# A decode block on one core: the second part of a late V is mixed one step later, and the down projection's weights lie in K's buffer

## The chip, the cores and the metric

The kernel runs on one core of one Trainium2 chip. The metric is the device time of an execution in microseconds (us); the kernel before took 1325.12 us in the median of three runs (1320.38 to 1325.15). The engines named below are TensorE (PE), VectorE (DVE), ScalarE (ACT) and SyncE (SP); nearly all transfers are issued from SP's queue, in program order.

## What is computed

One token for each of two sequences goes through a pre-norm attention block with a cache of 8192 keys and values in 16 heads of 256, and then through a gated projection without a nonlinearity:

```
# x: [2, 1, 448]; k_cache, v_cache: [2, 16, 8192, 256]; float32
q = layernorm(x) @ wq                        # 16 heads x 256
p = softmax(einsum("bhqd,bhkd->bhqk", q, k_cache) * 256 ** -0.5)
h = x + einsum("bhqk,bhkd->bhqd", p, v_cache) @ wo
n = layernorm(h)
out = h + ((n @ w_gate) * (n @ w_up)) @ w_down     # 448 -> 1792 -> 448
```

K and V of one head of one sequence are 8.39 MB each (8192 x 256 x 4 bytes), and there are 32 such pairs; all inputs together are 561 MB.

## The kernel before

**Tiling.** A pair i = 2 * head + sequence is one unit. The 8192 keys lie as 128 partitions x 64 rows (NJ = 64) of 256 elements, so a row of the buffer is 0.131 MB, and "16 rows" below are 2.10 MB. `k_sb` holds 112 rows: an even pair's K stands in rows 0 to 63, an odd pair's in rows 48 to 111. Both use rows 48 to 63, and every pair's `scores` begins with those 16 rows (for an even pair by taking part (part - 1) mod 4), so the next K may be loaded when the first of four parts has been reduced. `v_sb` holds a single V, 64 rows.

**A step.** The loop runs over n = 0 to 32. Step n loads V of pair n-1 and K of pair n+1, computes the scores of pair n, and the softmax and the mix (weights times V) of pair n-1. In program order: `load_v(n-1)`; `scores(n, 0)`, which multiplies 16 rows of K by q on DVE in place, calls `softmax(n-1)`, and then reduces those rows; `load_k(n+1)`; the other loads of V; a load of weights `w` in one step of four; `scores(n, 1)`, `norm(n-1)`, `scores(n, 2)` and `scores(n, 3)`; `mix(n-1)` and `mixed(n-1)`; `top(n)`. Each engine does its own instructions in this order; semaphores order them between engines.

**The pieces, with their lines.** `scores` is a product (L243) and a reduction (L246) on DVE for each of four parts. `top` takes the maximum over a row on DVE (L251) and transposes it on PE (L253, `mT`). `softmax` takes the maximum over the transposed row on DVE (L257, `nm`), spreads it by a matmul (L259), and makes the weights `p` and their sums on ACT (L264), which a matmul adds up (L268). `mix` is 32 matmuls (L279; each shows as two instructions in the profile) that add into one of two PSUM tiles `o_ps`, taken in turn; each reads two rows of V. `mixed` copies `o_ps` (ACT, L288), turns it into a column (PE, L292), scales it (ACT, L298) and, for the second sequence of a head, adds the output projection (PE, L301).

**The late steps.** For the last five pairs V is loaded in parts, by the table `LATE`: pair 27 in 56 + 8 rows, 28 in 48 + 16, 29 and 30 in 32 + 32, and 31 in 32 + 16 + 8 + 8. The first part is issued at the start of the step, the others behind `load_k(n+1)`.

**The end.** After the loop the gate's weights `wg` and the up projection's `wu` (3136 KB each) are loaded into rows of `k_sb`, and the down projection's `wd` into rows of `v_sb`, in three pieces (1792, 896 and 448 KB; L357). `project` multiplies the normed h by `wg` and by `wu` (both L379), and L438 multiplies by `wd` into `y_ps`, which DVE copies (L444) and two transfers store.

Of the kernel before, what the change touches and what calls it, by code (L numbers as in the profile page):

```python
# [13 lines left out]
B, D, H, SK, DH, F = 2, 448, 16, 8192, 256, 1792  # L14
# [5 lines left out]
NJ = SK // P  # L20
# [10 lines left out]
NF = F // P  # L31
# [13 lines left out]
def tile_decode_block(  # L45
# [8 lines left out]
    wd: bass.AP,  # L54
    out: bass.AP,
):

# [87 lines left out]
    def load_w(hp, lo=0, hi=WQ + 2 * WO):  # L147

        t = wpool.tile([P, WQ + 2 * WO], F32, tag="w", name=f"w_{hp}_{lo}")
        nc.sync.dma_start(t[:, lo:hi], w[hp][:, lo:hi])  # L150
        return t

    k_sb = const.tile([P, 2 * NJ - OVER, DH], F32, name="k_sb")
    v_sb = const.tile([P, NJ, DH], F32, name="v_sb")

    def keys_of(cache, i, lo, hi):
        h, b = divmod(i, B)
        return cache[b, h].rearrange("(p j) d -> p j d", p=P)[:, lo:hi, :]

    def k_at(i, lo, hi):  # L160
        base = i % 2 * (NJ - OVER)
        return k_sb[:, base + lo : base + hi, :]

    def load_k(i, lo=0, hi=NJ):
        nc.sync.dma_start(k_at(i, lo, hi), keys_of(k_cache, i, lo, hi))

    def load_v(i, lo=0, hi=NJ):
        nc.sync.dma_start(v_sb[:, lo:hi, :], keys_of(v_cache, i, lo, hi))
# [36 lines left out]
    def queries(hp, w):  # L205

        got = []
        for b in range(B):
            ps = ps_q.tile([P, 2 * DH], F32, tag="q", name=f"q_ps_{hp}_{b}")
            for c in range(DC - 1):  # L210
                nc.tensor.matmul(  # L211
                    ps, xb[:, c, b, :], w[:, c * 2 * DH : (c + 1) * 2 * DH],
                    start=(c == 0), stop=False,
                )
            for k in range(2):
                nc.tensor.matmul(  # L216
                    ps[:, k * DH : (k + 1) * DH], xb[:, DC - 1 + k, b, :],
                    w[:, 3 * 2 * DH : WQ], start=False, stop=(k == 1),
                )
            q = qpool.tile([P, 2, DH], F32, tag="q", name=f"q_{hp}_{b}")  # L220
            nc.scalar.activation(  # L221
                q.rearrange("p h d -> p (h d)"), ps, AF.Copy, scale=rstd[:, b : b + 1]
            )
            got.append(q)
        return got


    NQ = H * B
# [3 lines left out]
    def scores(i, part, between=None):  # L232

        h, b = divmod(i, B)
        if part == 0:
            s_t[i] = work.tile([P, NJ], F32, tag="s", name=f"s_{i}")

        lo = (part - 1) % (NJ // HC) * HC if i % 2 == 0 else part * HC  # L240
        kt = k_at(i, lo, lo + HC)
        q = q_t[h // 2][b][:, h % 2, :]
        nc.vector.tensor_mul(kt, kt, q[:, None, :].to_broadcast([P, HC, DH]))  # L243
        if between is not None:
            between()
        nc.vector.tensor_reduce(s_t[i][:, lo : lo + HC], kt, axis=AX.X, op=ALU.add)  # L246

    def top(i):

        m = work.tile([P, 1], F32, tag="m", name=f"m_{i}")  # L250
        nc.vector.tensor_reduce(m, s_t[i], axis=AX.X, op=ALU.max)  # L251
        mT_t[i] = ps_s.tile([1, P], F32, tag="sm", name=f"mT_{i}")
        nc.tensor.transpose(mT_t[i], m, ident)  # L253

    def softmax(i):
        nm = work.tile([1, 1], F32, tag="nm", name=f"nm_{i}")
        nc.vector.tensor_reduce(nm, mT_t[i], axis=AX.X, op=ALU.max, negate=True)  # L257
        nb_ps = ps_s.tile([P, 1], F32, tag="sm", name=f"nb_ps_{i}")
        nc.tensor.matmul(nb_ps, row, nm, start=True, stop=True)  # L259
        nb = work.tile([P, 1], F32, tag="nb", name=f"nb_{i}")  # L260
        nc.scalar.activation(nb, nb_ps, AF.Copy)  # L261
        p_t[i] = work.tile([P, NJ], F32, tag="p", name=f"p_{i}")
        lsum = work.tile([P, 1], F32, tag="lsum", name=f"lsum_{i}")
        nc.scalar.activation(  # L264
            p_t[i], s_t[i], AF.Exp, bias=nb, scale=DH**-0.5, accum_out=lsum
        )
        l_t[i] = ps_s.tile([P, 1], F32, tag="sm", name=f"l_ps_{i}")
        nc.tensor.matmul(l_t[i], ones, lsum, start=True, stop=True)  # L268

    def norm(i):  # L270
        rl_t[i] = work.tile([P, 1], F32, tag="rl", name=f"rl_{i}")
        nc.vector.reciprocal(rl_t[i], l_t[i])

    def mix(i):

        o, p = o_ps[i % 2], p_t[i]
        for t in range(NJ // 2):
            g = 32 * (t % 4)
            nc.tensor.matmul(  # L279
                o[g : g + 2, :], p[:, 2 * t : 2 * t + 2], v_sb[:, 2 * t : 2 * t + 2, :],  # L280
                start=(t < 4), stop=(t >= NJ // 2 - 4),
            )

    def mixed(i):

        h, b = divmod(i, B)
        o_sb = work.tile([P, 2 * DH], F32, tag="o_sb", name=f"o_sb_{i}")
        nc.scalar.activation(o_sb, o_ps[i % 2], AF.Copy)  # L288
        oT_ps = ps_s.tile([P, 2], F32, tag="sm", name=f"oT_ps_{i}")
        for c in range(2):  # L290
            for k in range(2):
                nc.tensor.matmul(  # L292
                    oT_ps[:, c : c + 1], o_sb[:, (2 * k + c) * P : (2 * k + c + 1) * P],
                    sel[:, k : k + 1], start=(k == 0), stop=(k == 1),
                )
        if b == 0:
            oT_t[h] = work.tile([P, 2, B], F32, tag="oT", name=f"oT_{h}")
        nc.scalar.activation(oT_t[h][:, :, b], oT_ps, AF.Copy, scale=rl_t[i])  # L298
        if b == B - 1:
            for c in range(2):  # L300
                nc.tensor.matmul(  # L301
                    acc_ps, oT_t[h][:, c, :], wo_t[h][:, c * D : (c + 1) * D],
                    start=(h == 0 and c == 0), stop=(h == H - 1 and c == 1),
                )

    for part in FIRST:
        load_k(0, *part)
    for n in range(NQ + 1):
        hp, at = divmod(n, 2 * B)
        late = n - 1 - (NQ - len(LATE))  # L310
        parts, todo = (LATE[late] if late >= 0 else (NJ,)) if n > 0 else (), []
        for k in range(len(parts)):
            todo.append((n - 1, sum(parts[:k]), sum(parts[: k + 1])))
        if n > 0:
            load_v(*todo.pop(0))
        if n < NQ:
            scores(n, 0, (lambda: softmax(n - 1)) if n > 0 else None)
        else:
            softmax(n - 1)
        if n + 1 < NQ:  # L320
            load_k(n + 1)
        for v in todo:
            load_v(*v)
        if at == 1:
            last = hp + 1 == H // 2
            t = load_w(hp + 1, lo=WQ, hi=WQ + WO) if last else load_w(hp + 1)
            w_t[hp + 1] = t
            for k in range(2):
                wo_t[2 * hp + k] = t[:, WQ + k * WO : WQ + (k + 1) * WO]
        if n == NQ:  # L330
            nc.sync.dma_start(wo_t[H - 1], w[H // 2][:, WQ + WO :])
        if n < NQ:
            scores(n, 1)
        if n > 0:
            norm(n - 1)
        if n < NQ:
            for part in range(2, NJ // HC):
                scores(n, part)
        if n > 0:
            mix(n - 1)  # L340
            mixed(n - 1)
        if at == 2 and hp + 1 < H // 2:
            q_t[hp + 1] = queries(hp + 1, w_t[hp + 1])
        if n < NQ:
            top(n)


    wg_t, wu_t = (
        k_sb.rearrange("p j d -> p (j d)")[:, k * NF * D : (k + 1) * NF * D] for k in range(2)
    )  # L350
    nc.sync.dma_start(wg_t, wg)
    nc.sync.dma_start(wu_t, wu)

    wd_t = v_sb.rearrange("p j d -> p (j d)")[:, : NF * D].rearrange("p (n d) -> p n d", d=D)
    at = 0
    for n in (8, 4, 2):
        nc.sync.dma_start(  # L357
# [150 lines left out]
```

## Time and profile before

| what | before |
|---|---|
| median of the runs | 1325.12 us |
| lowest and highest run | 1320.38, 1325.15 us |
| the profiled execution's own time | 1325.09 us |
| its span, first to last instruction | 1322.9 us |
| PE busy | 489.7 us (37%) |
| DVE busy | 1144.6 us (87%) |
| ACT busy | 62.3 us (5%) |
| bytes read, mean rate | 561.19 MB, 424 GB/s |
| mean granted clock of PE | 0.652 |

The profile is of one execution. In a row of the timeline the columns are the start, the time of one or of a merged run of instructions, the engine (SPq is SP issuing a transfer), the line, the operation, what it writes and reads, the count, and in brackets the idle time of that engine ahead of it with what ended it. In a row of the table by stretches there follow on the stretch and its length: busy time of PE, its weight loads, DVE, ACT and GpSimd, the granted clock of PE (1.00 is full), the busy share of the 16 DMA engines and the rate in GB/s. A row of a transfer gives its size and the time from its issue to its landing.

### The profile page before, as it was taken

Reading aid. Unit: us, or ns where it says so; the run is one execution under the profiler, and the core shown is the slowest. Engines: PE = TensorE matmul, PEld = TensorE weight load, DVE = VectorE, ACT = ScalarE, POOL = GpSimd, SP = SyncE. Lnnn points to the kernel's source line nnn. Section 1 sums busy time; section 2 is a strip of 40 time slices with the busy share of each in tenths; the row PEclk is TensorE's granted clock in tenths of the full one; section 3 lists DMA queues with packets and bytes.
Section 4 is the critical chain, followed back from the end, with each engine's and each line's share of the span. In section 5 each row is a group of like instructions: output and inputs, shape, how many; then the busy total and the mean of one; then the engine's idle time right before and its main releaser. Section 6 shows DMA issues by size and latency. Waiting matters only on the chain.

```text
span 1322.9 us, 6801 instructions
## 1 busy us (share of the span) xinstructions
PE 489.7 (37%) x2936; PEld 166.8 (13%) x2936; DVE 1144.6 (87%) x394; ACT 62.3 (5%) x183; POOL 1.2 (0%) x8
## 2 busy tenths in 40 slices
PE   3126333163331434324243451235332253243237
PEld 2012010020110211001010110012100020011013
DVE  7997999979998799897999989987999979979691
ACT  1000000000000000000000000000000000000000
POOL 0000000000000000000000000000000000000000
PEclk8567665576765866657666675667656686665668
DMA  9999999999999999999999999999999999999995
GB/s 408 444 434 421 434 440 430 428 434 439 428 431 436 438 430 429 423 450 428 434 434 430 431 438 431 432 434 429 434 439 426 433 432 433 432 392 394 424 426 219
DMA packets 12722, 561.62 MB, mean 425 GB/s; under 512 B 1427, under 2 KB 1429, under 8 KB 2069
## 3 DMA queue, kind: packets, MB, share of 16 engines
q1 hardware_dynamic: 12680, 561.19, 98.4%
q8 instruction: 23, 0.38, 0.1%
q14 instruction: 7, 0.05, 0.0%
q10 hardware_dynamic: 12, 0.01, 0.0%
HBM read 561.19 MB, written 0.00 MB: 424 GB/s over the span
## 4 chain that ended last, share of the span: by engine, by line
DMA 70%; DVE 25%; PE 4%; issue 1%; ACT 0%; SPq 0%; POOLq 0%; DVEq 0%; POOL 0%
DMA k_sb<-in_A_k_cache_dram 63%; DVE s L246 13%; DVE k_sb L243 12%; DMA v_sb<-in_A_v_cache_dram 7%; PE o_ps L279 2%; PE acc_ps L301 1%; PE oT_ps L292 0%; PE g_ps L379 0%; PE u_ps L379 0%; PE q_ps L198 0%; PE y_ps L438 0%; ACT o_sb L288 0%; DVE nm L257 0%; PE mT L253 0%; DVE xb L134 0%
## 5 line engine op out<-in xcount | busy, mean ns | idle before, releaser
L243 DVE TENSOR_TENSOR k_sb<-k_sb,q 128x4096 f32<-128x4096 f32 x128 | 564.9, 4414 | 119.7 <-DMA k_sb<-in_A_k_cache_dram 116.2
L246 DVE TENSOR_REDUCE s<-k_sb 128x16 f32<-128x4096 f32 x128 | 565.3, 4416 | 3.3
L279 PE MATMUL o_ps<-v_sb,p 128*2 128x512 f32 x2048 | 298.1, 745 | 455.2 <-DMA v_sb<-in_A_v_cache_dram 455.2
L279 PEld LDWEIGHTS o_ps<-v_sb,p 128*2 128x2 f32 x2048 | 53.7, 97 | 670.7 <-DMA v_sb<-in_A_v_cache_dram 461.7
L259 PE MATMUL nb_ps<-nm,row 1*128 1x1 f32 x64 | 16.9, 331 | 178.0 <-DVE nm L257 178.0
L253 PE MATMUL mT<-ident,m 128*1 128x128 f32 x32 | 10.7, 335 | 136.8 <-DVE m L251 136.8
L288 ACT ACTIVATE o_sb<-o_ps 128x512 f32<-128x512 f32 x32 | 19.1, 597 | 775.3 <-PE o_ps L279 775.3
L292 PE MATMUL oT_ps<-sel,o_sb 128*128 128x1 f32 x256 | 35.3, 259 | 23.2 <-ACT o_sb L288 23.2
L211 PE MATMUL q_ps<-w,xb 128*128 128x512 f32 x84 | 40.3, 616 | 0.0
L292 PEld LDWEIGHTS oT_ps<-sel,o_sb 128*128 128x128 f32 x256 | 32.6, 199 | 54.8 <-ACT o_sb L288 54.8
L301 PE MATMUL acc_ps<-w,oT 128*2 128x448 f32 x64 | 37.2, 718 | 5.6 <-ACT oT L298 5.6
L259 PEld LDWEIGHTS nb_ps<-nm,row 1*128 1x128 f32 x64 | 14.7, 283 | 187.2 <-issue 109.7
L268 PE MATMUL l_ps<-lsum,ones 128*128 128x1 f32 x64 | 17.9, 349 | 23.5 <-ACT p L264 23.5
L257 DVE TENSOR_REDUCE nm<-mT 1x1 f32<-1x128 f32 x32 | 8.7, 272 | 19.5 <-PE mT L253 19.5
L261 ACT ACTIVATE nb<-nb_ps 128x1 f32<-128x1 f32 x32 | 5.5, 171 | 351.0 <-PE nb_ps L259 351.0
L253 PEld LDWEIGHTS mT<-ident,m 128*1 128x1 f32 x32 | 2.6, 82 | 148.0 <-DVE m L251 114.2
L211 PEld LDWEIGHTS q_ps<-w,xb 128*128 128x128 f32 x84 | 16.1, 200 | 21.8 <-issue 21.4
L268 PEld LDWEIGHTS l_ps<-lsum,ones 128*128 128x128 f32 x64 | 15.2, 295 | 26.2 <-ACT p L264 26.2
L216 PE MATMUL q_ps<-w,xb 128*128 128x256 f32 x56 | 14.4, 379 | 0.0
L389 DVE TENSOR_TENSOR h_sb<-x_sb,acc_ps 2x448 f32<-2x448 f32 x1 | 0.6, 607 | 14.1 <-PE acc_ps L301 14.1
L221 ACT ACTIVATE q<-q_ps,rstd 128x512 f32<-128x512 f32 x14 | 9.6, 687 | 61.9 <-PE q_ps L216 61.9
L216 PEld LDWEIGHTS q_ps<-w,xb 128*128 128x128 f32 x56 | 10.6, 190 | 7.4 <-issue 6.7
(78 smaller groups left out, 100.4 us busy)
## 6 DMA issues: line engine op xcount, KB each, us to landing
v_sb<-in_A_v_cache_dram SPq DMA_DIRECT2D x5, 4096.0 KB, 23.2
w<-in_w_dram SPq DMA_DIRECT2D x7, 1792.0 KB, 33.7
v_sb<-in_A_v_cache_dram SPq DMA_DIRECT2D x1, 7168.0 KB, 27.6
v_sb<-in_A_v_cache_dram SPq DMA_DIRECT2D x1, 6144.0 KB, 29.6
k_sb<-in_A_k_cache_dram SPq DMA_DIRECT2D x2, 2048.0 KB, 13.5
k_sb<-in_A_k_cache_dram SPq DMA_DIRECT2D x1, 4096.0 KB, 22.8
v_sb<-in_A_v_cache_dram SPq DMA_DIRECT2D x2, 2048.0 KB
k_sb<-in_B_w_gate_dram SPq DMA_DIRECT2D x1, 3136.0 KB, 22.1
```

Source lines behind the costliest of these rows:

```text
L211: nc.tensor.matmul(ps, xb[:, c, b, :], w[:, c * 2 * DH : (c + 1) * 2 * DH], start=(c == 0), stop=False,)
L216: nc.tensor.matmul(ps[:, k * DH : (k + 1) * DH], xb[:, DC - 1 + k, b, :], w[:, 3 * 2 * DH : WQ], start=False, stop=(k == 1),)
L221: nc.scalar.activation(q.rearrange("p h d -> p (h d)"), ps, AF.Copy, scale=rstd[:, b : b + 1])
L243: nc.vector.tensor_mul(kt, kt, q[:, None, :].to_broadcast([P, HC, DH]))
L246: nc.vector.tensor_reduce(s_t[i][:, lo : lo + HC], kt, axis=AX.X, op=ALU.add)
L253: nc.tensor.transpose(mT_t[i], m, ident)
L259: nc.tensor.matmul(nb_ps, row, nm, start=True, stop=True)
L268: nc.tensor.matmul(l_t[i], ones, lsum, start=True, stop=True)
L279: nc.tensor.matmul(o[g : g + 2, :], p[:, 2 * t : 2 * t + 2], v_sb[:, 2 * t : 2 * t + 2, :], start=(t < 4), stop=(t >= NJ // 2 - 4),)
L288: nc.scalar.activation(o_sb, o_ps[i % 2], AF.Copy)
L292: nc.tensor.matmul(oT_ps[:, c : c + 1], o_sb[:, (2 * k + c) * P : (2 * k + c + 1) * P], sel[:, k : k + 1], start=(k == 0), stop=(k == 1),)
L301: nc.tensor.matmul(acc_ps, oT_t[h][:, c, :], wo_t[h][:, c * D : (c + 1) * D], start=(h == 0 and c == 0), stop=(h == H - 1 and c == 1),)
```

## The change

Two things are changed.

First, `mix` takes a range of rows. Where a step loads its V in two parts and a K is still to come (n = 28, 29 and 30, pairs 27, 28 and 29), the step ends with the mix of the first part only, and `(pair, lo, hi)` of the second part is kept in `rest`. The next step does that second part, and `mixed` of the pair, right behind its own softmax. Step 31 loads no further K, so pair 30 is mixed whole, as before, and so is pair 31 in step 32.

Second, `wd` takes the third stretch of 14 x 448 elements a partition in `k_sb`, behind `wg` and `wu` (rows 49 to 73), in place of the first stretch of `v_sb`.

```diff
--- before.py
+++ after.py
@@ -54,6 +54,7 @@
     wd: bass.AP,
     out: bass.AP,
 ):
+
 
 
 
@@ -271,10 +272,10 @@
         rl_t[i] = work.tile([P, 1], F32, tag="rl", name=f"rl_{i}")
         nc.vector.reciprocal(rl_t[i], l_t[i])
 
-    def mix(i):
+    def mix(i, lo=0, hi=NJ):
 
         o, p = o_ps[i % 2], p_t[i]
-        for t in range(NJ // 2):
+        for t in range(lo // 2, hi // 2):
             g = 32 * (t % 4)
             nc.tensor.matmul(
                 o[g : g + 2, :], p[:, 2 * t : 2 * t + 2], v_sb[:, 2 * t : 2 * t + 2, :],
@@ -305,6 +306,7 @@
 
     for part in FIRST:
         load_k(0, *part)
+    rest = None
     for n in range(NQ + 1):
         hp, at = divmod(n, 2 * B)
         late = n - 1 - (NQ - len(LATE))
@@ -317,6 +319,13 @@
             scores(n, 0, (lambda: softmax(n - 1)) if n > 0 else None)
         else:
             softmax(n - 1)
+        if rest is not None:
+            mix(*rest)
+            mixed(rest[0])
+            rest = None
+
+        if todo and n + 1 < NQ:
+            rest = todo[0]
         if n + 1 < NQ:
             load_k(n + 1)
         for v in todo:
@@ -337,21 +346,23 @@
             for part in range(2, NJ // HC):
                 scores(n, part)
         if n > 0:
-            mix(n - 1)
-            mixed(n - 1)
+            mix(n - 1, 0, rest[1] if rest is not None else NJ)
+            if rest is None:
+                mixed(n - 1)
         if at == 2 and hp + 1 < H // 2:
             q_t[hp + 1] = queries(hp + 1, w_t[hp + 1])
         if n < NQ:
             top(n)
 
 
-    wg_t, wu_t = (
-        k_sb.rearrange("p j d -> p (j d)")[:, k * NF * D : (k + 1) * NF * D] for k in range(2)
+
+    wg_t, wu_t, wd_t = (
+        k_sb.rearrange("p j d -> p (j d)")[:, k * NF * D : (k + 1) * NF * D] for k in range(3)
     )
     nc.sync.dma_start(wg_t, wg)
     nc.sync.dma_start(wu_t, wu)
 
-    wd_t = v_sb.rearrange("p j d -> p (j d)")[:, : NF * D].rearrange("p (n d) -> p n d", d=D)
+    wd_t = wd_t.rearrange("p (n d) -> p n d", d=D)
     at = 0
     for n in (8, 4, 2):
         nc.sync.dma_start(
```

The built programs show what moves. The first place is PE between the scores of steps 28 and 29. Before, from the sum of the weights of pair 27 (`l_ps`) on; `mT` is the transpose in `top(28)`, and `o_ps_98` the PSUM tile that pair 27 adds into:

```order
L268 MATMUL l_ps_2197<-lsum_2195,ones 128x1
L279 MATMUL o_ps_98<-v_sb,p_2194 2x512 x32
L292 MATMUL oT_ps_2244<-sel,o_sb_2242 128x1 x4
L301 MATMUL acc_ps<-w_0_1975,oT_2179 2x448 x2
L253 MATMUL mT_2254<-ident,m_2252 1x128
L259 MATMUL nb_ps_2261<-nm_2259,row 128x1
L268 MATMUL l_ps_2268<-lsum_2266,ones 128x1
```

After, the same stretch:

```order
L269 MATMUL l_ps_2197<-lsum_2195,ones 128x1
L280 MATMUL o_ps_98<-v_sb,p_2194 2x512 x28
L254 MATMUL mT_2240<-ident,m_2238 1x128
L260 MATMUL nb_ps_2247<-nm_2245,row 128x1
L269 MATMUL l_ps_2254<-lsum_2252,ones 128x1
L280 MATMUL o_ps_98<-v_sb,p_2194 2x512 x4
L293 MATMUL oT_ps_2263<-sel,o_sb_2261 128x1 x4
L302 MATMUL acc_ps<-w_0_1975,oT_2179 2x448 x2
```

The last 4 matmuls of mix 27, its column turn (L292, now L293) and the output projection have moved behind the three small matmuls of pair 28's maximum and softmax.

The second place is PE in steps 30 and 31. Before, from mix 29 on; `mT_2397` belongs to `top(30)` and `mT_2466` to `top(31)`:

```order
L279 MATMUL o_ps_98<-v_sb,p_2337 2x512 x32
L292 MATMUL oT_ps_2387<-sel,o_sb_2385 128x1 x4
L301 MATMUL acc_ps<-w_1792_2273,oT_2322 2x448 x2
L253 MATMUL mT_2397<-ident,m_2395 1x128
L259 MATMUL nb_ps_2404<-nm_2402,row 128x1
L268 MATMUL l_ps_2411<-lsum_2409,ones 128x1
L279 MATMUL o_ps_97<-v_sb,p_2408 2x512 x32
L292 MATMUL oT_ps_2457<-sel,o_sb_2455 128x1 x4
L253 MATMUL mT_2466<-ident,m_2464 1x128
L259 MATMUL nb_ps_2471<-nm_2469,row 128x1
```

After, from the first part of mix 29 on; `mT_2371` belongs to `top(30)` and `mT_2466` to `top(31)`:

```order
L280 MATMUL o_ps_98<-v_sb,p_2320 2x512 x16
L254 MATMUL mT_2371<-ident,m_2369 1x128
L260 MATMUL nb_ps_2378<-nm_2376,row 128x1
L269 MATMUL l_ps_2385<-lsum_2383,ones 128x1
L280 MATMUL o_ps_98<-v_sb,p_2320 2x512 x16
L293 MATMUL oT_ps_2406<-sel,o_sb_2404 128x1 x4
L302 MATMUL acc_ps<-w_1792_2273,oT_2341 2x448 x2
L280 MATMUL o_ps_97<-v_sb,p_2382 2x512 x32
L293 MATMUL oT_ps_2457<-sel,o_sb_2455 128x1 x4
L254 MATMUL mT_2466<-ident,m_2464 1x128
```

The second 16 matmuls of mix 29, its turn and the output projection now stand in step 31, ahead of mix 30, which is whole; ahead of `mT_2466` stand 48 matmuls of L280 since the softmax, where there were 32.

The third place is the end of SP's queue. Before:

```order
L331 DMA w_1792_2273<-in_w_dram 128x896
L351 DMA k_sb<-in_B_w_gate_dram 128x6272
L352 DMA k_sb<-in_B_w_up_dram 128x6272
L357 DMA v_sb<-in_wd_dram 128x3584
L357 DMA v_sb<-in_wd_dram 128x1792
L357 DMA v_sb<-in_wd_dram 128x896
```

After:

```order
L340 DMA w_1792_2273<-in_w_dram 128x896
L362 DMA k_sb<-in_B_w_gate_dram 128x6272
L363 DMA k_sb<-in_B_w_up_dram 128x6272
L368 DMA k_sb<-in_wd_dram 128x3584
L368 DMA k_sb<-in_wd_dram 128x1792
L368 DMA k_sb<-in_wd_dram 128x896
```

The order is the same; the three pieces of `wd` go to `k_sb`. Before, they waited for the matmuls of mix 31 that read those rows of V; now they wait for reductions of pair 31's K.

## The prediction

> **What bounds the kernel now.** I read the page first, for what is busy and for the chain that ended last.
>
> ```profile
> span 1322.9 us, 6801 instructions
> q1 hardware_dynamic: 12680, 561.19, 98.4%
> DMA 70%; DVE 25%; PE 4%; issue 1%; ACT 0%; SPq 0%; POOLq 0%; DVEq 0%; POOL 0%
> L257 DVE TENSOR_REDUCE nm<-mT 1x1 f32<-1x128 f32 x32 | 8.7, 272 | 19.5 <-PE mT L253 19.5
> ```
>
> One queue moves 561 MB and is busy for 98.4% of the span, so over the whole kernel the transfers are the limit. The last row speaks against "nothing else matters": VectorE (DVE) stood 19.5 us in front of the small reduction of L257, which needs TensorE's (PE's) transpose mT. The timeline of DVE says where: the rows below open steps 29, 30 and 31 (each step's first product with K), and give L257's wait in each; the last ends the scores of step 31.
>
> ```profile
> 1160.09 4.42 DVE L243 TENSOR_TENSOR k_sb<-k_sb,q 128x4096 f32<-128x4096 f32 x1 [0.61 <-DMA k_sb<-in_A_k_cache_dram]
> 1170.90 0.28 DVE L257 TENSOR_REDUCE nm<-mT 1x1 f32<-1x128 f32 x1 [6.38 <-PE mT L253]
> 1202.10 4.42 DVE L243 TENSOR_TENSOR k_sb<-k_sb,q 128x4096 f32<-128x4096 f32 x1
> 1208.78 0.28 DVE L257 TENSOR_REDUCE nm<-mT 1x1 f32<-1x128 f32 x1 [2.26 <-PE mT L253]
> 1239.98 4.42 DVE L243 TENSOR_TENSOR k_sb<-k_sb,q 128x4096 f32<-128x4096 f32 x1
> 1254.79 0.28 DVE L257 TENSOR_REDUCE nm<-mT 1x1 f32<-1x128 f32 x1 [10.40 <-PE mT L253]
> 1285.85 0.22 DVE L251 TENSOR_REDUCE m<-s 128x1 f32<-128x64 f32 x1
> ```
>
> 6.38 + 2.26 + 10.40 = 19.04 us, all in the steps whose V comes in two parts. PE's timeline gives the cause: mixes (L279) that wait for V.
>
> ```profile
> 1162.59 1.88 PE L279 MATMUL o_ps<-v_sb,p 128*2 128x512 f32 x8 [14.35 <-DMA v_sb<-in_A_v_cache_dram]
> 1177.10 7.24 PE L279 MATMUL o_ps<-v_sb,p 128*2 128x512 f32 x48 [4.38 <-DMA v_sb<-in_A_v_cache_dram]
> 1202.33 3.59 PE L279 MATMUL o_ps<-v_sb,p 128*2 128x512 f32 x16 [17.99 <-DMA v_sb<-in_A_v_cache_dram]
> 1213.16 6.26 PE L279 MATMUL o_ps<-v_sb,p 128*2 128x512 f32 x32 [2.08 <-DMA v_sb<-in_A_v_cache_dram]
> 1245.11 5.64 PE L279 MATMUL o_ps<-v_sb,p 128*2 128x512 f32 x32 [25.70 <-DMA v_sb<-in_A_v_cache_dram]
> 1256.55 3.62 PE L279 MATMUL o_ps<-v_sb,p 128*2 128x512 f32 x32
> 1265.70 5.59 PE L279 MATMUL o_ps<-v_sb,p 128*2 128x512 f32 x32 [5.54 <-DMA v_sb<-in_A_v_cache_dram]
> 1286.13 0.37 PE L253 MATMUL mT<-ident,m 128*1 128x128 f32 x1 [13.05 <-DVE m L251]
> 1288.76 9.44 PE L279 MATMUL o_ps<-v_sb,p 128*2 128x512 f32 x64
> ```
>
> The second parts (x8, x16, x32 at 1162.59, 1202.33, 1245.11) land only after the next K, and mT stands behind them in PE's queue. DVE's stall then delays the transfers too: K(n+1) goes into rows that DVE's first reduce of step n frees, and SP's queue shows it, since K30 and K31 were issued as those reduces ended; the third row is the second half of V30, issued when the mix that began at 1245.11 was over.
>
> ```profile
> 1175.53 0.33 SPq L165 DMA_DIRECT2D k_sb<-in_A_k_cache_dram  x1
> 1213.41 0.33 SPq L165 DMA_DIRECT2D k_sb<-in_A_k_cache_dram  x1
> 1250.83 0.33 SPq L168 DMA_DIRECT2D v_sb<-in_A_v_cache_dram  x1
> ```
>
> The table by stretches shows the queue running dry at both places; the last column is GB/s.
>
> ```profile
> 1172.00:1176.00 4.00, 0.38 (x2) 0.30 (x2) 4.00 (x2) 0.29 (x2) 0.00 (x0) 0.77 0.34 147
> 1212.00:1220.00 8.00, 6.26 (x32) 0.99 (x32) 7.96 (x3) 0.00 (x0) 0.00 (x0) 0.59 0.76 287
> 1220.00:1304.00 84.00, 34.51 (x202) 9.45 (x202) 56.61 (x23) 3.80 (x12) 0.00 (x0) 0.67 1.00 428
> 1304.00:1308.00 4.00, 2.81 (x28) 1.58 (x32) 2.12 (x14) 0.00 (x0) 0.00 (x0) 0.91 0.73 298
> ```
>
> **The change part by part.** Nothing before 1160 moves: steps 0 to 28 load and compute as before, but for the last 8 instructions of mix 27.
>
> *DVE.* mT of steps 28, 29, 30 now stands ahead of the second part of the mix, behind a first part whose V landed long before (1177.1 and 1213.2 against scores that end near 1196 and 1232). The three stalls go. What is late next is K. K30 landed 4.9 us ahead of V28's second part (2.10 MB at 428 GB/s), so at 1202.3 - 4.9 = 1197.4. Its issue moves up 6.4 us, but V28's first part still fills the queue until 1177.1, so K30 gains only the dry spell: 0.7 to 2.6 us (below); I take 0.7, landing 1196.7. DVE alone would be ready at 1202.1 - 6.4 = 1195.7, so step 30 opens at 1196.7. A step without stall takes 1239.98 - 1202.10 - 2.26 = 35.6 us, so step 31 opens at 1232.3 (K31, 1245.1 - 9.8 = 1235.3 now, needs to come 3 us earlier; it does, by the next paragraph). Step 31 costs 1286.07 - 1239.98 - 10.40 = 35.7: scores end at **1268.0, 18.1 us earlier**.
>
> *Transfers.* The dry spells are counted in two ways. By rate against 428: 4 x (1 - 147/428) = 2.6 and 8 x (1 - 287/428) = 2.6, together 5.3. By landings: K30 and V28's second part, 10.49 MB, took 1177.1 to 1202.3 = 25.2 where 428 GB/s needs 24.5; K31 and V29's second part, 12.58 MB, took 1213.2 to 1245.1 = 31.9 where 29.4 would do: together 3.2. With K30 issued 6.4 us and K31 7.5 us earlier, both come while the queue still has V in it, so neither spell is left. I take the middle, **4.3 us**, ends 0 and 5.3 (more than the spells hold can't be won: the bytes stay).
>
> By the Trainium skill ("DMA: Bandwidth & Descriptors", Anatomy of one DMA) a transfer has about 2.0 us of fixed cost beside its bytes; two exposed starts would make an estimate of 4.0 us, and the time 0.3 us longer than mine.
>
> *PE and SP.* The second part's 8, 16 and 32 instructions cost what they did (1.9, 3.6, 5.6 us) and now lie beside DVE's reduces, with the softmax ahead of them. Queued behind them: V's next second part must wait for them. A step's product takes 4.4 us, the softmax 2.6 (mT at 1286.13 to the mix at 1288.76): V28's second part is released near 1160.1 + 4.4 + 2.6 + 1.9 = 1169.0, V29's near 1196.7 + 4.4 + 2.6 + 3.6 = 1207.3, and the queue then has K30 (to 1196.7) or K31 (to 1231.0) still moving, so that wait is covered by over 20 us. The load of w in step 29 waits for the output projection of mix 27, now near 1174, under the same cover. V30's second half is released by the mix that V29's landing starts, as before. In step 31 PE does mix 29's rest, all of mix 30 with its column turn (L292), then mT.
>
> ```profile
> 1272.02 1.05 PE L292 MATMUL oT_ps<-sel,o_sb 128*128 128x1 f32 x8 [0.73 <-ACT o_sb L288]
> ```
>
> V30's second half lands at 1265.7 - 4.3 = 1261.4; now from the mix's start at 1265.70 to the end of that turn at 1273.07 are 7.4 us, so mT stands at 1268.8: 0.8 us of new wait.
>
> *The end.* mix 31 starts 2.6 us after mT, at 1271.4, and takes 9.4, to 1280.8. With nothing else in the way it would end 17.4 us ahead of 1298.2. But V31 and the weights come last now.
>
> ```profile
> 1272.70 0.44 SPq L352 DMA_DIRECT2D k_sb<-in_B_w_up_dram  x1
> w<-in_w_dram SPq DMA_DIRECT2D x1, 448.0 KB, 14.6
> k_sb<-in_B_w_gate_dram SPq DMA_DIRECT2D x1, 3136.0 KB, 22.1
> k_sb<-in_B_w_up_dram SPq DMA_DIRECT2D x1, 3136.0 KB, 28.9
> 1311.39 4.04 PE L379 MATMUL u_ps<-k_sb,xr 128*32 128x256 f32 x62
> 1319.70 0.28 DVE L444 COPY y<-y_ps 128x112 f32<-128x112 f32 x1 [2.65 <-PE y_ps L438]
> SPq L357 <- PE o_ps L279: 18.6, 3, 17.0
> 1292.40 2.71 SPq L357 DMA_DIRECT2D v_sb<-in_wd_dram  x3
> ```
>
> The up weights landed at 1272.70 + 28.9 = 1301.6, 9.8 us before u used them. Less 4.3 they land at 1297.3. Behind V31's last part the queue has the last w, gate and up, 6.88 MB or 16.1 us, so V31 is there at 1281.2; an x8 takes 1.9, and mix 31 ends at 1283.1. From its end to u were 1311.39 - 1298.2 = 13.2 us, so PE is ready for u at 1296.3 and waits 1.0 us. From u's start to the copy of y are 8.3 us, and 3.2 to the end: 1297.3 + 8.3 + 3.2 = **1308.8**.
>
> *wd in K's rows.* It removes the 18.6 us that SP waited for mix 31, but until 1304 the queue was full (428 GB/s), so that wait cost nothing before; after it wd is issued behind the up weights at once, and its bytes end at 1304 + 2.8 - 4.3 = 1302.5, by when y needs its first part (1297.3 + 5.4). I cost it at 0. With wd still in V's rows it would be issued 3.6 us (1288.76 to 1292.40) into mix 31, at 1275, while the queue is full to 1297: no cost either, so no cover is lost.
>
> **Sum.** The profiled run took 1325.09 for a span of 1322.9, 2.2 us around it, and is the median (1325.12) itself. 1308.8 + 2.2 = **1311.0**.
>
> **Rivals.**
> - *The dry spells only move* (late V or K loads leave the same gaps elsewhere). For it: part of the lost rate may be a straggling end of a transfer. Then the up weights stay at 1301.6: 1301.6 + 11.5 + 2.2 = 1315.3. Chance 0.16.
> - *A cold PE at the end.* After idling 25.70 and 5.54 us the same x32 took 5.64 and 5.59, without idling 3.62. If PE's wait for the up weights is long enough to lose the clock, u takes 4.04 x 1.54 = 6.2: 1313.2. Against it: the wait I expect is 1 us. Chance 0.13. The Trainium skill ("TensorE: Matmul & The Clock Gate", Part 1) has the clock fall to half after an idle window of about 3.4 us, free-running; by that rule 1 us does not suffice, and the trace's 5.54 us agrees.
> - *Transfers gain as much as DVE* (a faster stretch than 428): the whole 18.5 us, 1306.6. Against it: the bytes after 1177 are unchanged. Chance 0.08.
> - *The stall comes back.* mT of step 31 behind mix 30, or K late by 10 us; or mT was not what DVE lacked: 1320 to 1325. Against it: the rows of PE above. Chance 0.09.
> - *Slower: SP is held by the moved mix.* V29's second part, and behind it all of V30, V31 and the weights, wait for the rest of mix 28. If this came free only with the softmax of step 31 (near 1239), K31's end at 1231 would leave the queue dry for some 10 us, and the same at V30's second half: 1311 + 20 = 1331. It decides from a release later than 1231; I expect 1207, so 24 us of margin. Chance 0.04.
>
> **How the numbers follow.** Forecast 0.50, the rest as above. The range 1305 to 1316.5 holds the forecast, the cold PE, the moved spells and most of the full gain, and leaves out the returning stall and the slower case, with a little of each edge. 0.5%, about what a measurement can tell here, is 6.6 us: faster is below 1318.5. Forecast and first three rivals fall there: 0.87; the returning stall is within: 0.09; slower 0.04.
>
> **What would show it.** Right: L257's waits in steps 29 to 31 gone; K30 and K31 issued near 1169 and 1206, no stretch below 400 GB/s between 1177 and 1300; the last scores near 1268; PE waiting for the up weights before u. Wrong: a wait of DVE on K of over 3 us in step 30 or 31, a dry stretch near 1231 or 1242, or a wait of PE on mT's place in step 31.

## The result, and the profile after

The changed kernel took 1311.24 us in the median of six runs (1310.35 to 1312.84) against 1325.13 us before (1320.38 to 1326.29): 13.9 us less, a ratio of 0.9905 with a 95% interval of 0.9886 to 0.9925. The runs of the kernel before lie in two groups, 1319.8 to 1321.3 and 1323.1 to 1326.3 us in all jobs, and its profile is of the upper one, so against the lower one the gain is about 9 us, and no trace tells what differs between them. The profiled run took 1310.35 us for a span of 1308.1; the forecast was 1311.0 and 1308.8.

The page of the changed kernel, in the lines shown of before (span, queue, chain by engine):

```profile
span 1308.1 us, 6800 instructions
q1 hardware_dynamic: 12680, 561.19, 99.4%
DMA 73%; DVE 23%; PE 3%; issue 0%; ACT 0%; POOLq 0%; DVEq 0%; POOL 0%
```

The same bytes fill 99.4% of a shorter span. From the waits of DVE between 1160 and 1322, the row of the reduction that had stood 19.5 us, and then DVE's timeline where steps 29, 30 and 31 open, with the end of the last scores (lines are one higher than before):

```profile
DVE nm L258 <- PE mT L254: 1.1, 1, 1.1
```

```profile
1160.04 4.42 DVE L244 TENSOR_TENSOR k_sb<-k_sb,q 128x4096 f32<-128x4096 f32 x1 [0.61 <-DMA k_sb<-in_A_k_cache_dram]
1164.38 0.27 DVE L258 TENSOR_REDUCE nm<-mT 1x1 f32<-1x128 f32 x1
1196.40 4.43 DVE L244 TENSOR_TENSOR k_sb<-k_sb,q 128x4096 f32<-128x4096 f32 x1 [0.74 <-DMA k_sb<-in_A_k_cache_dram]
1200.75 0.27 DVE L258 TENSOR_REDUCE nm<-mT 1x1 f32<-1x128 f32 x1
1231.95 4.42 DVE L244 TENSOR_TENSOR k_sb<-k_sb,q 128x4096 f32<-128x4096 f32 x1
1236.28 0.27 DVE L258 TENSOR_REDUCE nm<-mT 1x1 f32<-1x128 f32 x1
1267.35 0.22 DVE L252 TENSOR_REDUCE m<-s 128x1 f32<-128x64 f32 x1
1268.67 0.28 DVE L258 TENSOR_REDUCE nm<-mT 1x1 f32<-1x128 f32 x1 [1.10 <-PE mT L254]
```

The three stalls are gone: L258 follows its product without a bracket. What is left is 0.74 us on K30 and, at the end, 1.10 us on mT of step 31. The scores end 18.5 us earlier (1267.35 against 1285.85, the start of their last maximum), but the span shrinks by 14.8. SP's queue and the table by stretches say where the rest went:

```profile
1169.02 0.33 SPq L166 DMA_DIRECT2D k_sb<-in_A_k_cache_dram  x1
1205.38 0.33 SPq L166 DMA_DIRECT2D k_sb<-in_A_k_cache_dram  x1
1268.17 0.47 SPq L363 DMA_DIRECT2D k_sb<-in_B_w_up_dram  x1
k_sb<-in_B_w_up_dram SPq DMA_DIRECT2D x1, 3136.0 KB, 28.3
```

```profile
1172.00:1176.00 4.00, 2.51 (x4) 0.26 (x2) 3.96 (x2) 0.00 (x0) 0.00 (x0) 0.50 0.95 410
1212.00:1220.00 8.00, 6.41 (x32) 0.99 (x32) 7.96 (x4) 0.00 (x0) 0.00 (x0) 0.64 1.10 475
1220.00:1224.00 4.00, 0.00 (x0) 0.00 (x0) 4.00 (x2) 0.00 (x0) 0.00 (x0) 0.66 0.76 328
1220.00:1300.00 80.00, 47.29 (x310) 15.59 (x312) 51.46 (x35) 4.49 (x13) 0.00 (x0) 0.68 0.98 415
```

K30 and K31 are issued 6.5 and 8.0 us earlier, the two dry spells (147 and 287 GB/s) are gone (410 and 475), and the up weights land at 1268.17 + 28.3 = 1296.5, 5.1 us earlier. They can't gain as much as DVE does, since the same bytes have to be moved. Three landings, at which PE's mixes of V29's first and second part and of V30's first half begin, are used further down:

```profile
1212.16 6.41 PE L280 MATMUL o_ps<-v_sb,p 128*2 128x512 f32 x32 [3.08 <-DMA v_sb<-in_A_v_cache_dram]
1241.23 5.53 PE L280 MATMUL o_ps<-v_sb,p 128*2 128x512 f32 x32 [2.72 <-DMA v_sb<-in_A_v_cache_dram]
1250.96 3.62 PE L280 MATMUL o_ps<-v_sb,p 128*2 128x512 f32 x32 [0.40 <-DMA v_sb<-in_A_v_cache_dram]
```

The end of PE's timeline:

```profile
1280.51 1.04 PE L280 MATMUL o_ps<-v_sb,p 128*2 128x512 f32 x8 [0.98 <-DMA v_sb<-in_A_v_cache_dram]
1284.12 3.15 PE L302 MATMUL acc_ps<-w,oT 128*2 128x448 f32 x4 [0.35 <-ACT oT L299]
1290.35 1.92 PE L390 MATMUL g_ps<-k_sb,xr 128*32 128x512 f32 x8 [0.50 <-DVE xr L135]
1292.72 4.12 PE L390 MATMUL g_ps<-k_sb,xr 128*32 128x512 f32 x22
1296.56 0.41 PE L390 MATMUL u_ps<-k_sb,xr 128*32 128x256 f32 x2
1296.80 3.91 PE L390 MATMUL u_ps<-k_sb,xr 128*32 128x256 f32 x62
```

The gate's two rows before:

```profile
1306.10 1.05 PE L379 MATMUL g_ps<-k_sb,xr 128*32 128x512 f32 x8 [0.50 <-DVE xr L134]
1307.79 3.76 PE L379 MATMUL g_ps<-k_sb,xr 128*32 128x512 f32 x22
```

mix 31 ends at 1281.55, after waiting for V31's last part, and u begins right behind the gate's products (L390 into `g_ps`), its main run at 1296.8, 0.3 us behind the landing of the up weights. No bracket stands ahead of u: in this execution PE's own chain came last, but by so little that a PE ahead by more than 0.3 us would have waited for the up weights. Two limits nearly meet there.

### The profile page after: what moved, and what is told of

It reads as the page before. It is cut to its first block, busy times and chain, and to the rows that moved or that the text cites. A ratio compares the mean times of both kernels' runs of the same rounds, so it can differ in the third digit from the quotient of the medians.

```text
span 1308.1 us, 6800 instructions
## 1 busy us (share of the span) xinstructions
PE 492.3 (38%) x2936; PEld 169.0 (13%) x2936; DVE 1144.4 (87%) x394; ACT 62.3 (5%) x183; POOL 1.2 (0%) x8
## 3 DMA queue, kind: packets, MB, share of 16 engines
q1 hardware_dynamic: 12680, 561.19, 99.4%
## 4 chain that ended last, share of the span: by engine, by line
DMA 73%; DVE 23%; PE 3%; issue 0%; ACT 0%; POOLq 0%; DVEq 0%; POOL 0%
DMA k_sb<-in_A_k_cache_dram 68%; DVE k_sb L244 11%; DVE s L247 11%; DMA v_sb<-in_A_v_cache_dram 5%; PE o_ps L280 1%; PE g_ps L390 0%; PE u_ps L390 0%; PE q_ps L199 0%; PE acc_ps L302 0%; PE y_ps L449 0%; DVE nm L258 0%; PE oT_ps L293 0%; DVE xb L135 0%; DVE o_ps L102 0%; PE hm_ps L442 0%
## 5 line engine op out<-in xcount | busy, mean ns | idle before, releaser
L280 PE MATMUL o_ps<-v_sb,p 128*2 128x512 f32 x2048 | 298.2, 745 | 401.6 <-DMA v_sb<-in_A_v_cache_dram 401.6
L280 PEld LDWEIGHTS o_ps<-v_sb,p 128*2 128x2 f32 x2048 | 53.6, 97 | 616.5 <-DMA v_sb<-in_A_v_cache_dram 408.7
L293 PE MATMUL oT_ps<-sel,o_sb 128*128 128x1 f32 x256 | 35.8, 261 | 23.2 <-ACT o_sb L289 23.2
L293 PEld LDWEIGHTS oT_ps<-sel,o_sb 128*128 128x128 f32 x256 | 33.1, 202 | 54.8 <-ACT o_sb L289 54.8
L265 ACT ACTIVATE p<-s,nb 128x64 f32<-128x64 f32 x32 | 11.1, 347 | 1.0
```

The costliest lines, as they stand in the source:

```text
L265: nc.scalar.activation(p_t[i], s_t[i], AF.Exp, bias=nb, scale=DH**-0.5, accum_out=lsum)
L280: nc.tensor.matmul(o[g : g + 2, :], p[:, 2 * t : 2 * t + 2], v_sb[:, 2 * t : 2 * t + 2, :], start=(t < 4), stop=(t >= NJ // 2 - 4),)
L293: nc.tensor.matmul(oT_ps[:, c : c + 1], o_sb[:, (2 * k + c) * P : (2 * k + c + 1) * P], sel[:, k : k + 1], start=(k == 0), stop=(k == 1),)
```

## The experiments

All ratios are against runs of the kernel before in the same job. That kernel's median was 1325.13 us in the job of the result and 1323.58, 1320.52 and 1324.35 us in the three jobs below; since it moves by up to 4.6 us, a kernel's own median is given beside its ratio.

### The deferred mix alone

```diff
-wd_t = wd_t.rearrange("p (n d) -> p n d", d=D)
+wd_t = v_sb.rearrange("p j d -> p (j d)")[:, : NF * D].rearrange("p (n d) -> p n d", d=D)
```

The third stretch of `k_sb` is not taken either (not shown).

> The deferred mix alone, wd back in V's rows. Theory A (the mix does it all): 1311 us, as with both edits; wd is issued about 3.6 us into mix 31, near 1275, still ahead of the end of the up weights near 1296. Rival B (the place of wd gives part of it): 1314 us or more, with wd landing after y is ready for it.

Measured: 1310.53 us (1310.18 to 1310.92), ratio 0.9899 (0.9875 to 0.9924). SP's row for wd in that run:

```profile
1272.43 3.31 SPq L368 DMA_DIRECT2D v_sb<-in_wd_dram  x3
```

wd is issued from 1272.4 on, 24 us ahead of the end of the up weights that stand in front of it. The time is that of both edits (1311.24 us) within the scatter of the runs, so the mix gives all of the gain that can be told.

### wd in K's rows alone

The mix as before, `wd_t` as the third stretch of `k_sb`.

> wd in K's rows alone, the mix as before. Theory A: no change, 1320 to 1326 us; the wait of SP for mix 31 (18.6 us) goes, and the end does not move, since DVE's chain ends last. Rival B: faster by over 2 us.

Measured: 1321.91 us (1319.67 to 1325.17), ratio 0.9987 (0.9971 to 1.0003): no difference that can be told, though the interval would hide one of up to 3.8 us. SP's row for wd in that run:

```profile
1269.83 10.96 SPq L357 DMA_DIRECT2D k_sb<-in_wd_dram  x3
```

wd is issued from 1269.83 on, where SP had stood until 1292.40, and the span is 1322.9, as before. Removing an 18.6 us wait of an engine's queue did not move the end, since the transfers ahead of it had not ended.

### Only pair 29's second half late

```diff
-        if todo and n + 1 < NQ:
+        if todo and n == 30:
```

> Only pair 29's second half is mixed late (step 31); pairs 27 and 28 are mixed as before. The 10.4 us stall goes, the stalls of 6.4 and 2.3 us and the late issue of K30 and K31 stay. Theory A (two limits, DVE's chain and the transfers): the scores end at 1286.1 - 10.4 = 1275.7, the up weights land at 1301.6 as before, and u waits for them: 1315.3 us. Rival C (every us of stall is a us of time): 1325.1 - 10.4 = 1314.7 us, with u starting when PE is ready and no wait for the up weights. The time hardly tells them apart; the landing of the up weights and the idle time of PE ahead of u do.

Measured: 1316.63 us (1313.62 to 1317.05), ratio 0.9940 (0.9917 to 0.9963). DVE's rows of the two stalls left in, and PE at the end of that run:

```profile
1171.00 0.28 DVE L258 TENSOR_REDUCE nm<-mT 1x1 f32<-1x128 f32 x1 [6.37 <-PE mT L254]
1207.79 0.28 DVE L258 TENSOR_REDUCE nm<-mT 1x1 f32<-1x128 f32 x1 [1.17 <-PE mT L254]
```

```profile
1301.33 3.65 PE L390 MATMUL u_ps<-k_sb,xr 128*32 128x256 f32 x64 [1.71 <-DMA k_sb<-in_B_w_up_dram]
1307.16 1.72 PE L449 MATMUL y_ps<-k_sb,hmT 128*2 128x112 f32 x64 [0.79 <-DMA k_sb<-in_wd_dram]
1309.26 1.59 PE L449 MATMUL y_ps<-k_sb,hmT 128*2 128x112 f32 x48 [0.38 <-DMA k_sb<-in_wd_dram]
```

The first stall is as before, the second 1.17 us where it was 2.26. The brackets at the end name the limit: PE stands 1.71 us for the up weights, which land where they did before (1301.3), and 1.17 us for wd. The scores end at 1274.4, 11.5 us earlier, and the span is 8.8 us shorter: the difference is what the unmoved transfers keep back. So the sum of the stalls is not the rule. As expected, the time does not tell the theories apart: the median is 1.3 us over what I had for two limits, about the 1.17 us of wd that I had left out, and 1.9 us over rival C.

### Only pairs 27 and 28 late

```diff
-        if todo and n + 1 < NQ:
+        if todo and n in (28, 29):
```

> Only pairs 27 and 28 are mixed late; pair 29 is mixed whole in step 30. The stalls of 6.4 and 2.3 us go and K30 and K31 are issued 6.4 and 8 us earlier, so the transfers gain the dry spells (the up weights land near 1297). Theory A: step 31 opens at 1232 but V29's second half lands only at 1241.2, so its stall grows from 10.4 to about 14.5 us; the scores end near 1282.2 and the time is 1321.2 us. Rival C (sum of the stalls): 1325.1 - 8.6 = 1316.5 us.

Measured: 1320.71 us (1317.42 to 1321.31), ratio 0.9980 (0.9967 to 0.9992). DVE's row for step 31:

```profile
1250.60 0.28 DVE L258 TENSOR_REDUCE nm<-mT 1x1 f32<-1x128 f32 x1 [14.15 <-PE mT L254]
```

Two stalls of 6.38 and 2.26 us were removed, and the third grew from 10.40 to 14.15 us: DVE arrives earlier and waits for the same landing of V29. The scores end at 1281.9 (1282.2 expected). The median lies at theory A's 1321.2, not at rival C's 1316.5, so this tells the two apart by time as well.

### Pair 30 late too

```diff
-        if todo and n + 1 < NQ:
+        if todo and n < NQ:
```

> Pair 30 is mixed late too: its second half behind the softmax of step 32, so the rule is carried one step further. Theory A (the release of V's rows decides, the forecast's slower rival at another place): V31's second part may be issued only when that mix has read rows 32 to 47, near 1273.4, but V31's first part lands at 1270.4 and nothing else is queued, so the queue runs dry for 4 to 5 us and all that lands behind is as much later: 1315.5 us, with a stretch near 1272 well below 400 GB/s. Rival C (only DVE's stall counts): the 0.8 us that mT waits in step 31 goes, 1310.4 us.

Measured: 1317.25 us (1316.89 to 1318.47), 6.0 us more than the change in its own job; ratio to before 0.9967 (0.9955 to 0.9979). PE's row for the moved part of mix 30, and the table by stretches of that run:

```profile
1270.35 6.09 PE L280 MATMUL o_ps<-v_sb,p 128*2 128x512 f32 x32
```

```profile
1264.00:1268.00 4.00, 0.22 (x1) 0.08 (x1) 3.69 (x2) 0.00 (x0) 0.00 (x0) 0.50 0.99 426
1268.00:1272.00 4.00, 2.89 (x13) 1.25 (x16) 0.61 (x3) 0.61 (x3) 0.00 (x0) 0.50 0.15 66
1272.00:1276.00 4.00, 4.00 (x28) 0.68 (x20) 0.00 (x0) 0.00 (x0) 0.00 (x0) 0.58 0.28 74
1276.00:1280.00 4.00, 3.27 (x36) 1.49 (x32) 0.00 (x0) 0.86 (x2) 0.00 (x0) 1.00 1.01 422
```

This is the slower rival of the prediction, at the place where its point is passed: V31's second part waits for rows that the moved mix reads and is issued at 1274.0, in the middle of that mix (1273.4 expected), nothing else is queued, and the rate falls to 66 and 74 GB/s: 4 x (1 - 66/428) + 4 x (1 - 74/428) = 6.7 us lost, which covers the difference. The mechanism was as expected; the time came out 1.7 us above the 1315.5 expected.

### What holds the end: three cuts

First, an eighth of the up weights:

```diff
-    nc.sync.dma_start(wu_t, wu)
+    nc.sync.dma_start(wu_t[:, : NF * D // 8], wu[:, : NF * D // 8])
```

> Only the first eighth of the up weights' columns is loaded (the rest of the product uses what stands in K's rows), so they land some 6 us earlier. Theory D (at the end PE's own chain from V31's last part is as late as the up weights): within 0.5 us of 1311. Theory E (the forecast: the up weights are last, by 1 us): 1310 us, u starting 1 us earlier.

Second, `mix` of pair 31 without the last 8 rows, with the up weights whole:

```diff
-                start=(t < 4), stop=(t >= NJ // 2 - 4),
+                start=(t < 4), stop=(t >= (NJ - 8 * (i == NQ - 1)) // 2 - 4),
...
-            mix(n - 1, 0, rest[1] if rest is not None else NJ)
+            mix(n - 1, 0, rest[1] if rest is not None else NJ - 8 * (n == NQ))
```

> The last 8 rows of V31 are loaded but left out of mix 31, so PE's chain at the end starts about 2.0 us earlier. Theory D: PE then stands 1.5 to 2 us idle in front of u until the up weights land, and the time is within 0.5 us of 1311. Theory F (PE's chain alone decides): 1309.2 us.

Third, both:

> The two cuts together: an eighth of the up weights, and mix 31 without V31's last 8 rows. Theory D: both limits move, 2.0 us faster than with either alone, 1309.2 us (span about 1306.1). If a third limit is close behind (the gate's weights, or wd), less.

Measured: 1311.55 us (1308.93 to 1311.89), 1310.73 us (1310.04 to 1310.92) and 1309.14 us (1308.42 to 1309.85); ratios to before 0.9930 (0.9909 to 0.9951), 0.9922 (0.9905 to 0.9940) and 0.9911 (0.9893 to 0.9929). The medians of either cut alone are within about 0.5 us of the change's 1311.24, that of both is 2.1 us below it. The change was not run in this job, and its ratio, 0.9905, does not show that gain, because the kernel before was 4.6 us faster in the median here. Within the job every run with both cuts was shorter than every run with the second alone; one run with the first alone, 1308.93 us, lies among those with both.

PE's rows of the second cut, and then of both:

```profile
1289.87 1.92 PE L390 MATMUL g_ps<-k_sb,xr 128*32 128x512 f32 x8 [3.23 <-DMA k_sb<-in_B_w_gate_dram]
1297.24 3.65 PE L390 MATMUL u_ps<-k_sb,xr 128*32 128x256 f32 x64 [1.20 <-DMA k_sb<-in_B_w_up_dram]
```

```profile
1289.49 1.92 PE L390 MATMUL g_ps<-k_sb,xr 128*32 128x512 f32 x8 [1.76 <-DMA k_sb<-in_B_w_gate_dram]
```

With PE's chain shortened, PE waits for the gate's weights and then for the up weights; with those cut too, the gate is the third limit, close behind. The profile of the first cut is of its 1308.93 us run, 2.4 us ahead of the other three:

```profile
1290.04 1.05 PE L390 MATMUL g_ps<-k_sb,xr 128*32 128x512 f32 x8 [0.50 <-DVE xr L135]
1295.35 4.04 PE L390 MATMUL u_ps<-k_sb,xr 128*32 128x256 f32 x62
```

There the granted clock was 0.93 from 1288 to 1292, where the change had 0.50. The gate's first 8 instructions took 1.05 us, not 1.92, and u's main run began 13.1 us after mix 31 (which ended at 1282.25), not 15.25. So how near the two limits lie depends on the clock that PE was granted. In both traces of the change, at 0.50, PE reached u 0.3 us behind the up weights (1296.8 and 1296.5; 1298.1 and 1297.8 in the second trace), and a faster PE alone would have won no more than that. The first cut's other three runs took about what the lower clock would give, but they have no trace, so this is not shown.

### Two versions that compute everything

Gate and up weights in two transfers each, split behind half of their chunks, and V31's end as 4 + 4 rows:

```diff
-LATE = ((56, 8), (48, 16), (32, 32), (32, 32), (32, 16, 8, 8))
+LATE = ((56, 8), (48, 16), (32, 32), (32, 32), (32, 16, 8, 4, 4))
...
-    nc.sync.dma_start(wg_t, wg)
-    nc.sync.dma_start(wu_t, wu)
+    for t, src in ((wg_t, wg), (wu_t, wu)):
+        for lo, hi in ((0, 2 * F), (2 * F, NF * D)):
+            nc.sync.dma_start(t[:, lo:hi], src[:, lo:hi])
```

> A version that keeps the whole computation: gate and up weights are each loaded in two pieces, so that their first chunks can be used when half has landed, and the last 8 rows of V31 come as 4 + 4, so that fewer matmuls stand behind the last landing. Theory D (two limits at the end, tied): both ease by 0.5 to 1.2 us, 1310.3 us. If PE at half clock decides alone: only the 0.5 us of the shorter last part. If the further transfers cost anything: 1311.5 or more.

The same, with `keep` called in four gaps of PE behind mix 31:

```diff
+    def keep(i):
+        if i == NQ - 1:
+            nc.tensor.matmul(o_ps[0][0:2, :], ones[:, 0:2], v_sb[:, 0:2, :], start=True, stop=True)
```

> As the split version, with four further matmuls of 2 x 512 into an accumulator that nobody reads any more, in the gaps of PE behind mix 31, to keep its clock up. If the half clock between mix 31 and the gate's products is due to those gaps, they run some 2 us faster and the time is 1309 us; if not, the four matmuls only take room (up to 0.85 us each) and it is 1311 us or more.

And the changed kernel beside them:

> The changed kernel itself beside the two: 1311.2 us, between 1310.3 and 1312.9.

Measured: 1310.19 us (1310.11 to 1312.59), 1311.74 us (1310.62 to 1313.90) and 1311.72 us (1311.43 to 1311.92); ratios 0.9904 (0.9886 to 0.9922), 0.9912 (0.9895 to 0.9928) and 0.9909 (0.9892 to 0.9926). The ranges overlap, so none of them is shown to be faster. The second version's stretch behind mix 31, its wait in the middle of u, and that for wd:

```profile
1288.00:1292.00 4.00, 3.56 (x27) 1.09 (x25) 2.57 (x13) 0.00 (x0) 0.00 (x0) 1.00 1.02 435
1292.00:1296.00 4.00, 3.40 (x31) 1.42 (x34) 0.32 (x2) 0.69 (x1) 0.00 (x0) 1.00 1.00 424
```

```profile
1299.04 2.78 PE L397 MATMUL u_ps<-k_sb,xr 128*32 128x256 f32 x48 [2.15 <-DMA k_sb<-in_B_w_up_dram]
1305.62 1.58 PE L458 MATMUL y_ps<-k_sb,hmT 128*2 128x112 f32 x48 [0.53 <-DMA k_sb<-in_wd_dram]
```

The clock is full there (1.00, where the changed kernel had 0.50), and PE spends what it wins in front of the up weights' second piece and of wd. So the 1309 us expected of a full clock did not come: with the queue at 424 to 435 GB/s, the faster PE of this run only waited longer.

## Why the prediction was right, point by point

- **The cause of the stalls.** Right, and shown: with mT ahead of the second part L258 waits for nothing in steps 29 and 30 and at step 31's opening, and each experiment that puts second parts back brings their stalls back.
- **DVE's chain.** Right: openings of steps 30 and 31 at 1196.7 and 1232.3 were forecast, 1196.4 and 1231.95 came; the scores end at 1267.6 (1268.0). For mT in step 31 a new wait of 0.8 us was forecast, and L258 showed 1.10.
- **The transfers' gain.** The term was 4.3 us with ends 0 and 5.3; the up weights came 5.1 us earlier, near the upper end, the count by rate. The Trainium skill ("DMA: Bandwidth & Descriptors", Anatomy of one DMA) gives the 2.0 us, which the prediction sets beside this term, for transfers that GpSimd issues, while these are SP's; the estimate of 4.0 us made from it lies 1.1 us below what came. The sign "no stretch below 400 GB/s" was too sharp: several stretches of 4 us lie below it, 1220 to 1224 at 328 and those from 1244 to 1252 at 369. By landings nothing was lost there: K31 and V29's second part, 12.58 MB, came from 1212.2 to 1241.2, in 29.1 us (31.9 before), 433 GB/s, and V30's first half behind them, landing at 1250.9, took 9.7 us for 4.19 MB, 432 GB/s. The rate of so short a stretch is not that of the landings.
- **wd.** 0 us forecast, and neither edit alone shows another cost, within the interval given above.
- **The end.** Here a step was wrong. The forecast had the up weights last, by 1.0 us, and PE waiting for them; PE did not wait, and its own chain was last by 0.3 us. The term at fault is the 13.2 us from mix 31 to u, taken over from before: it took 15.25 us. At a granted clock of 0.50 the gate's first 8 instructions took 1.92 us (before 1.05), its 22 next ones 4.12 (3.76), and the small steps ahead of the gate 0.9 us more.
- **The sum, and luck in it.** u began 0.5 us earlier than the 1297.3 of the sum. That is partly luck: mix 31 ended 1.55 us earlier than worked out (1281.55, not 1283.1), PE's chain from there took 2.05 us longer, and the up weights came 0.8 us earlier. The median's agreement, 1311.24 with 1311.0, is closer than the scatter of the six runs, 2.5 us, can bear out.
- **The rivals.** The cold PE did appear, but behind mix 31 rather than in front of u, and the landing of the up weights left it no more than 0.3 us of cost. The spells did not move. SP held by the moved mix did not decide here (V's second parts were released at 1168.4 and 1206.5, against 1169.0 and 1207.3 worked out) and did decide one pair later, at 6 us.

## What to carry to other kernels

PE did its matmuls in the order of the program here, so a short step that another engine waits for should not stand behind work that waits for a late transfer: put the late work behind it, and check who needs the buffer that the late work still reads. A stall that goes is worth its length only until the next limit, and a second stall of the same kind downstream can take it all back, so follow both the waiting engine and the queue that it feeds. A wait in a queue whose earlier transfers still run did not move the end here.

## What the runs showed of the hardware that I had not expected

The clock of PE (the last column but two) does not follow from the busy share in the tables by stretches. First the changed kernel behind mix 31, then the split version:

```profile
1284.00:1288.00 4.00, 3.18 (x5) 0.37 (x5) 0.70 (x2) 0.07 (x1) 0.00 (x0) 0.50 0.99 427
1288.00:1292.00 4.00, 3.24 (x22) 1.27 (x22) 1.88 (x12) 0.00 (x0) 0.00 (x0) 0.50 1.02 439
1292.00:1296.00 4.00, 4.00 (x24) 1.81 (x24) 0.32 (x2) 0.00 (x0) 0.00 (x0) 0.50 0.95 405
```

```profile
1280.00:1284.00 4.00, 2.86 (x16) 1.18 (x15) 0.00 (x0) 0.86 (x2) 0.00 (x0) 1.00 1.00 424
1284.00:1288.00 4.00, 2.35 (x22) 0.90 (x22) 1.68 (x8) 0.00 (x0) 0.00 (x0) 1.00 1.02 433
```

The clock was 0.50 with PE busy 3.18 to 4.00 us of 4, and 1.00 with 2.86 and 2.35. The four further matmuls came with 1.00 throughout in the one profile taken, which does not show that they were the cause. The Trainium skill ("TensorE: Matmul & The Clock Gate", Part 1) has the clock fall after an idle window of about 3.4 us; here it fell to 0.50 near 1283 with no gap of PE above 0.98 us since 1270.89, so that rule alone does not account for it. What decides it stays open.
